# Strided attention feeding two token-mixing layers on one core: the softmax of batches 1 and 2 is transposed two steps behind its scores instead of one

## The chip, the cores and the metric

The kernel runs on one core of a Trainium2 chip. Five engines work side by side, each through its own queue in order: TensorE (PE in the rows; PEld is its weight load), VectorE (DVE), ScalarE (ACT), GpSimd (POOL) and SyncE (SP), which here issues nearly all DMA transfers. The metric is the device time of one execution in microseconds; it is given as the median over several runs, beside the span of one profiled execution.

## The reference

Four batches (B = 4) of 576 tokens and 8 heads of 64 channels go through three layers. All inputs are float32.

```
scores = q k^T / sqrt(64);  heads 0-3 keep 0 <= i-j < 32, heads 4-7 keep j <= i, j = i (mod 32)
attn   = exp(scores - max) / (sum + 1e-9);  x = attn v, heads side by side       (576 x 512)
h = relu(x w_in); u, v = halves of h; v_n = (v - mean) / sqrt(var + 1e-6)
x2 = (u * (w_spatial v_n + b)) w_out                                             (576 x 512)
th = x2 w_theta;  y = w_tok_r (x2 cos th) + w_tok_i (x2 sin th);  s = x2 + y
out = s + relu(s w_ch)
```

The second and third layer are dense; every batch passes through the same weights. The attention is sparse: a local head needs a band of 32 keys per query, and a strided head, after its tokens are permuted, is block diagonal with small triangles.

## The kernel before, in words

**The main work.** Dense products run in float16 in three passes (high x high, low x high, high x low parts), because one float16 pass is not exact enough. For every batch b the generator `main_v(b)` computes v (tiles `v`) and normalizes it into `vn`; `main_mid(b)` computes u (`u`), the spatial product (`sp`), x2 (tiles `x`) and theta (`th`) with sine and cosine (tiles `ta`); `main_end(b)` computes y (`y`) and the last product (`c`). They run in the order v(0), mid(0), v(1), end(0), mid(1), v(2), end(1), and so on, so v of the next batch stands behind th of this one. `main_v(b)` reads the attention's output `xT` of batch b: four chunks of 128 channels (two heads each), each as a high part, written by ScalarE, and a low part, written by VectorE as source minus high part. The weights arrive as raw 64-bit floats; they are turned to float32 and split by ScalarE, VectorE and GpSimd while batch 0 is in `main_mid` (tiles `x2f`, `zf`, `xT_94` as staging, `wx` and `x2h` in between, `wout`, `wth`, `wtok`, `wch` as results).

**The attention of batches 1 and 2** is the generator `attention1(b)` (line 810), in float32. Its blocks of 64 or 54 queries are grouped in eight `quads`: five local (heads 0 to 3), then three strided, of which the middle one mixes two head pairs. A step s does up to four things. `qd_scores` writes the scores and masks of quad s into a PSUM tile `a`, taken from the same three buffers (`pm`) that the tiles u, sp, x, th, v, y and c take. `qd_softmax` (line 745) has VectorE take the maximum (`st`) and subtract it (`sm`), and ScalarE take the exponential in place; `qd_div` divides by the sum on VectorE. `qd_turn` transposes `sm` on TensorE into the one PSUM bank `av`, and ScalarE copies it to `pT`. `qd_px` multiplies `pT` with v into the bank `sc` (strided quads: `sc` and `av`), and `gr_parts` copies the result into `xT`, the high part on ScalarE, then the low part on VectorE. Before, step s held scores(s), turn(s-1) and px(s-2).

**What sets the order.** Python generators are advanced by a clock that counts the columns of the main matmuls: step n of the attention of a batch starts at `ATT_AT[b][0] + n * ATT_AT[b][1]` (line 57: 2.7 + 4.2 n for batch 1, 86.0 + 5.4 n for batch 2). `main_v(b)` is not begun before the attention of b is drained. A list scheduler then orders the instructions of each engine: first come those with the higher priority, and by program order otherwise; calls through `hv`, `ha`, `hg` (line 166) count as 200 instructions earlier (`AHEAD`). Nearly all evacuations of the main work go through these; the maximum and the subtraction of `qd_softmax` did not. DMA transfers wait in one SyncE queue; `load_b(hp)` issues 4 transfers for a local and 13 for a strided pair of v.

All compute is recorded through helper functions, so every row of the profile shows the same line, L107; rows are told apart by their tiles.

Of the kernel before, what the change touches and what calls it, by code (L numbers as in the profile page):

```python
# [14 lines left out]
F32 = mybir.dt.float32  # L15
# [4 lines left out]
ALU = mybir.AluOpType  # L20
# [49 lines left out]
def kernel(  # L70
# [52 lines left out]
    nc = Engines  # L123
# [18 lines left out]
    P = 128  # L142
# [23 lines left out]
    hv, ha, hg = Ahead(nc.vector, AHEAD), Ahead(nc.scalar, AHEAD), Ahead(nc.gpsimd, AHEAD)  # L166
# [12 lines left out]
    att_p = ctx.enter_context(tc.tile_pool(name="att", bufs=1))  # L179
# [43 lines left out]
    def pm(name):  # L223
        return ps_m.tile([P, 2, 512], F32, tag="pm", name=name)

    def pa(tag):
        return ps_a.tile([P, 512], F32, tag=tag, name=tag)

    def pa4(tag):
        return pa(tag).rearrange("p (n k) -> p n k", n=4)  # L230
# [227 lines left out]
    def load_qk(b, hp, q, k, c0, c1, by=None):  # L458
        by = by or nc.sync
        local = hp < 2  # L460
        src = kzl[b, hp] if local else kzs[b, hp - 2]
        k0, k1 = (c0 + STRIDE if c0 else 0, c1 + STRIDE) if local else (c0, c1)
        by.dma_start(q[:, c0:c1], qp[b, hp][:, c0:c1])
        for j in range(2):
            h = slice(64 * j, 64 * j + 64)
            by.dma_start(k[h, k0:k1], src[h, j, k0:k1])
# [155 lines left out]
    def gr_parts(b, local, blocks, xt, by=1):  # L622

        xh = xT[b % 2]
        runs = []
        for i, (hp, blk) in enumerate(blocks):
            if runs and runs[-1][0] == hp and (local or blk < 10):
                runs[-1][3] += 1
            else:
                runs.append([hp, blk, i, 1])  # L630
        for hp, blk, i, n in runs:
            src = xt[:, QB * i:QB * (i + n)]
            if local:
                dst = [xh[:, e, hp, QB * blk:QB * (blk + n)] for e in range(2)]
            else:
                nr = min(3, STRIDE - 3 * blk)
                r0, o = (3 * (blk - blk % by), blk % by) if nr == 3 else (3 * blk, 0)
                dst = [xh[:, e, hp, :].rearrange("p (j r) -> p j r", r=STRIDE)
                       [:, :, r0:r0 + n * nr * (by if nr == 3 else 1)]
                       .rearrange("p j (n t r) -> p j n t r", n=n, r=nr)[:, :, :, o] for e in range(2)]  # L640
                src = src.rearrange("p (n c) -> p n c", c=QB)[:, :, 0:nr * NCLS].rearrange(
                    "p n (r j) -> p j n r", j=NCLS)
            nc.scalar.activation(dst[0], src, AF.Copy)
            nc.vector.tensor_tensor(dst[1], src, dst[0], ALU.subtract)
# [61 lines left out]
    NQ = len(quads)  # L706

    def qd_size(g):
        local, slots = quads[g]
        return local, slots, len(slots), 96 if local else QB  # L710
# [34 lines left out]
    def qd_softmax(g, sc, sm, st):  # L745
        local, slots, ns, w = qd_size(g)
        n = 2 * ns
        sv = sc[:, :, 0:ns * w].rearrange("p j (n c) -> p j n c", c=w)
        mx = st[:, 0, 0:n].rearrange("p (j n) -> p j n", j=2)
        nc.vector.tensor_reduce(out=mx, in_=sv, op=ALU.max, axis=mybir.AxisListType.X)  # L750
        nc.vector.tensor_tensor(sm[:, 0:n * w].rearrange("p (j n c) -> p j n c", j=2, c=w), sv,
                                mx.unsqueeze(3).broadcast_to([P, 2, ns, w]), ALU.subtract)
        nc.scalar.activation(sm[:, 0:n * w], sm[:, 0:n * w], AF.Exp, scale=0.125)

    def qd_div(g, sm, st):

        local, slots, ns, w = qd_size(g)
        n = 2 * ns
        p, sums = sm[:, 0:n * w].rearrange("p (n c) -> p n c", c=w), st[:, 1, 0:n]
        nc.vector.tensor_reduce(out=sums, in_=p, op=ALU.add, axis=mybir.AxisListType.X)  # L760
        nc.vector.tensor_scalar(sums, sums, 1e-9, 1.0 / XS, op0=ALU.add, op1=ALU.mult)
        nc.vector.reciprocal(sums, sums)
        nc.vector.tensor_tensor(p, p, sums.unsqueeze(2).broadcast_to([P, n, w]), ALU.mult)

    def qd_places(g):


        local, slots, ns, w = qd_size(g)
        if local:
            return [f * w for f in range(2 * ns)], lambda j, s: (j * ns + s, 0)  # L770
        odd = ns % 2
        starts = []
        for j in range(2):
            starts += [j * ns * w] * odd + [(j * ns + s) * w for s in range(odd, ns, 2)]
        half = len(starts) // 2
        return starts, lambda j, s: (j * half + (s + odd) // 2, 64 * ((s + odd) % 2) if s or not odd else 0)

    def qd_turn(g, sm, pt, pT):
        local = quads[g][0]
        w, n = (96, P)[not local], len(qd_places(g)[0])  # L780
        for t, c in enumerate(qd_places(g)[0]):
            nc.tensor.transpose(pt[0:w, t, :], sm[:, c:c + w], ident)
        nc.scalar.activation(pT[0:w, 0:n], pt[0:w, 0:n], AF.Copy)

    def qd_px(b, g, v, pT):


        local, slots, ns, w = qd_size(g)
        place = qd_places(g)[1]
        banks = (pa("sc"),) if local else (pa("sc"), pa("av"))  # L790
        held = [[] for _ in banks]
        for s, slot in enumerate(slots):
            for half, (hp, blk) in enumerate(slot):
                e = 0 if local else blk % 2
                m = QB if local else min(CB, S - CB * blk)
                o = QB * len(held[e])
                held[e].append((hp, blk))
                for j in range(2):
                    t, r = place(j, s)
                    q = slice(64 * half, 64 * half + m)  # L800
                    if local:
                        lhs, rhs = v[hp][0:96, blk, 64 * j:64 * j + 64], pT[0:96, t, q]
                    else:
                        assert r == 64 * e
                        lhs, rhs = v[hp][r:r + m, blk // 2, 64 * j:64 * j + 64], pT[r:r + m, t, q]
                    nc.tensor.matmul(banks[e][64 * j:64 * j + 64, o:o + m], lhs, rhs, start=True, stop=True)
        for e in range(len(banks)):
            gr_parts(b, local, held[e], banks[e], len(banks))

    def attention1(b):  # L810
        q, k, v = {}, {}, {}

        def load_a(hp):
            q[hp], k[hp] = kts[hp % 2][:, 0], kts[hp % 2][:, 1]
            load_qk(b, hp, q[hp], k[hp], 0, S)

        def load_b(hp):
            v[hp] = att_p.tile([P, 9, P], F32, tag="vT", name="v32", bufs=2)
            if hp < 2:
                load_vl(b, hp, v[hp])  # L820
            else:
                load_vs(b, v[hp][:, 0:6].unsqueeze(1), (hp,))

        load_a(0)
        load_b(0)
        yield
        load_a(1)
        load_b(1)
        loads = {2: (load_a, 2), 4: (load_a, 3), 5: (load_b, 2), 6: (load_b, 3)}
        un = {}  # L830
        for s in range(NQ + 2):
            def turn():
                sm, pT, st = un[s - 1]
                qd_turn(s - 1, sm, pa4("av"), pT)

            if s == NQ:
                turn()
            if s >= 2:
                sm, pT, st = un.pop(s - 2)
                qd_px(b, s - 2, v, pT)  # L840
            if s < NQ:
                sm = att_p.tile([P, 512], F32, tag="sm", name="sm", bufs=2)
                pT = att_p.tile([P, 4, P], F32, tag="pT", name="pT32", bufs=2)
                st = att_p.tile([P, 2, 8], F32, tag="st", name="st", bufs=4)
                un[s] = (sm, pT, st)
                sc = pm("a1")
                qd_scores(s, q, k, sc)
                qd_softmax(s, sc, sm, st)
            if s in loads:
                f, hp = loads[s]  # L850
                f(hp)
            if 1 <= s < NQ:
                turn()
            if s < NQ:
                qd_div(s, *un[s][::2])
            yield


# [373 lines left out]
    timed([lambda n=n: tok_step(n) for n in range(len(toks))], *CONV_TOK)  # L1232
    timed(sq_parts(wch, w_ch, 2), *CONV_CH)
    atts = [None] + [attention1(b) for b in range(1, N32)] + [attention(b) for b in range(N32, B)]
    for at, f in [(at, lambda n=n: tok_load(*toks[n])) for n, at in enumerate(TOK_AT)] + [
            (at, lambda: next(atts[N32])) for at in PREP_AT]:
# [148 lines left out]
```

## Time and profile before

| | |
|---|---|
| median of 3 runs | 496.44 us (493.58 to 498.56) |
| the profiled execution | 493.71 us, its span 491.9 us |
| TensorE busy | 470.0 us, 96% of the span |
| VectorE, ScalarE, GpSimd busy | 300.8, 268.4, 72.6 us |
| attention of batch 1 in the span | about 36 to 112 us, beside v(0) and mid(0) |
| attention of batch 2 in the span | about 158 to 227 us |

In the profile's page the span is cut in 40 equal slices of 12.3 us. TensorE's share is six to nine tenths in the first eight of them, up to 98 us, and nine tenths or more from there to the last slice. VectorE and ScalarE are mostly five to nine tenths busy up to about 150 us and mostly less than half later, VectorE with exceptions. Where TensorE waits, the trace names the engine and tile whose result came last.

### The profile page before, as it was taken

To read this page: it belongs to the slowest core of one execution; us is meant where nothing else is said; L and a number is where in the kernel's file an instruction comes from. 1 tells how busy PE (TensorE), PEld (TensorE's weight loads), DVE (VectorE), ACT (ScalarE), POOL (GpSimd) and SP (SyncE) were. 2 spreads that over 40 slices of the span, in tenths; PEclk is the share of its full clock that TensorE was granted. 3 is DMA by queue.
4 is the path that set the end of the run, shared out by engine and by line. 5 is a ranking of instruction groups with operands and counts; after the bars stand their busy time and mean duration, and the time that the engine had idled before them with its cause. 6 is when DMAs were issued, how large, how long until landed. Compare 5 with 4: busy or idle time off the path is not lost. (4 is left out here: it accounts for less than half of the span.)

```text
span 491.9 us, 10785 instructions
## 1 busy us (share of the span) xinstructions
PE 470.0 (96%) x4440; PEld 353.6 (72%) x4440; DVE 300.8 (61%) x639; ACT 268.4 (55%) x480; POOL 72.6 (15%) x69
## 2 busy tenths in 40 slices
PE   7889869799999999999999999999999999999996
PEld 5655647567477777777668877777667777777775
DVE  4766987966898655762688778862687121217412
ACT  2657777878974334444955657654952022148202
POOL 2041144120004300111004110021005200210320
PEclk9999979999999999999999999999999999999999
DMA  6887647465890064200282255230360020003502
GB/s 178 284 228 219 206 166 220 161 227 130 220 199 1 0 211 133 59 26 1 49 218 85 57 151 158 45 65 1 47 147 1 2 97 0 1 2 73 121 0 98
DMA packets 71820, 52.72 MB, mean 107 GB/s; under 512 B 50584, under 2 KB 59992, under 8 KB 71770
## 3 DMA queue, kind: packets, MB, share of 16 engines
q1 hardware_dynamic: 71466, 51.42, 38.1%
q8 instruction: 35, 0.57, 0.5%
q10 hardware_dynamic: 304, 0.61, 0.4%
q14 instruction: 15, 0.12, 0.1%
HBM read 35.36 MB, written 4.72 MB: 81 GB/s over the span
## 5 line engine op out<-in xcount | busy, mean ns | idle before, releaser
L107 PE MATMUL y<-wtok,zf 128*128 128x288 f16 x864 | 107.2, 286 | 0.0
L107 PEld LDWEIGHTS <-zf 128*128 128x128 f16 x864 | 84.1, 98 | 22.2 <-issue 1.2
L107 PE MATMUL sp<-wsp,vn 128*128 128x288 f16 x384 | 51.5, 291 | 1.7 <-ACT vn L107 1.7
L107 PE MATMUL u<-xT,win 128*128 128x288 f16 x384 | 50.3, 289 | 2.0 <-DVE sm L107 2.0
L107 PEld LDWEIGHTS <-vn 128*128 128x128 f16 x416 | 41.0, 99 | 12.6 <-ACT vn L107 1.9
L107 PE MATMUL v<-win,xT 128*128 128x512 f16 (+1 forms) x240 | 48.6, 380 | 1.2 <-POOL win L107 0.6
L107 PE MATMUL x<-zf,wout 128*128 128x288 f16 x384 | 49.6, 286 | 0.0
L107 PE MATMUL th<-x2h,wth 128*128 128x288 f16 x384 | 47.8, 286 | 0.0
L107 POOL TENSOR_TENSOR x2h<-x2f,x2h 128x576 f16<-128x576 f32 x19 | 26.2, 1383 | 141.9 <-issue 66.0
L107 PEld LDWEIGHTS <-win 128*128 128x128 f16 x384 | 37.8, 99 | 11.8 <-DVE sm L107 2.3
L107 PE MATMUL c<-x2h,wch 128*128 128x288 f16 x360 | 45.2, 286 | 0.0
L107 PEld LDWEIGHTS <-wth 128*128 128x128 f16 x384 | 37.6, 98 | 9.6 <-issue 0.2
L107 PEld LDWEIGHTS <-wch 128*128 128x128 f16 x384 | 37.5, 98 | 9.2
L107 PEld LDWEIGHTS <-wout 128*128 128x128 f16 x384 | 36.8, 98 | 9.5
L107 PEld LDWEIGHTS <-xT 128*128 128x128 f16 (+1 forms) x240 | 21.0, 100 | 25.7 <-issue 2.8
L107 ACT ACTIVATE x2h<-x2f 128x576 f16<-128x576 f32 (+1 forms) x28 | 20.9, 748 | 24.9 <-DVE x2f L107 23.5
L107 ACT ACTIVATE o<-c 128x576 f32<-128x576 f32 x15 | 9.7, 645 | 34.9 <-PE c L107 34.7
L107 DVE TENSOR_TENSOR ta<-ta,x2f 128x1152 f32<-128x1152 f32 (+1 forms) x17 | 21.7, 1283 | 11.2 <-ACT ta L107 11.2
L107 DVE SCALAR_TENSOR_TENSOR x2f<-y,x2f 128x576 f32<-128x576 f32 x16 | 12.0, 752 | 25.4 <-PE y L107 25.3
L107 POOL TENSOR_TENSOR zf<-u,zf 128x576 f16<-128x576 f32 x8 | 10.2, 1280 | 113.9 <-ACT zf L107 109.4
L107 DVE TENSOR_TENSOR u<-u,sp 128x576 f32<-128x576 f32 x16 | 12.0, 751 | 24.5 <-PE sp L107 24.5
L107 DVE SCALAR_TENSOR_TENSOR o<-x2f,o 128x576 f32<-128x576 f32 (+1 forms) x17 | 12.2, 722 | 23.7 <-ACT o L107 23.7
(146 smaller groups left out, 724.9 us busy)
## 6 DMA issues: line engine op xcount, KB each, us to landing
out_dram<-o SPq DMA_DIRECT2D x15, 288.0 KB
kt<-in_qp_dram SPq DMA_DIRECT2D x8, 288.0 KB
qs<-in_qd_dram SPq DMA_DIRECT2D x8, 288.0 KB
x2f<-in_w_in_dram SPq DMA_DIRECT2D x2, 1024.0 KB
zf<-in_w_in_dram SPq DMA_DIRECT2D x2, 1024.0 KB
xT<-in_w_ch_dram SPq DMA_DIRECT2D x2, 1024.0 KB
kt<-in_kzl_dram SPq DMA_DIRECT2D x8, 152.0 KB
ks<-in_kl_dram SPq DMA_DIRECT2D x4, 304.0 KB
```

The costliest lines, as they stand in the source:

```text
L107: ins = f(*args, **kwargs)
```

## The change

In `attention1` step s now holds px(s-3), scores(s) and turn(s-2), so a batch takes eleven steps instead of ten, on the same clock. For this, `sm` gets four buffers (the tag `ph`, unused at that time, takes every second one), `pT` is taken when it is needed, and the last load of v moves from step 6 to step 7. In `qd_softmax`, the maximum and the subtraction are issued with priority.

```diff
-        nc.vector.tensor_reduce(out=mx, in_=sv, op=ALU.max, axis=mybir.AxisListType.X)
-        nc.vector.tensor_tensor(sm[:, 0:n * w].rearrange("p (j n c) -> p j n c", j=2, c=w), sv,
+        hv.tensor_reduce(out=mx, in_=sv, op=ALU.max, axis=mybir.AxisListType.X)
+        hv.tensor_tensor(sm[:, 0:n * w].rearrange("p (j n c) -> p j n c", j=2, c=w), sv,
                                 mx.unsqueeze(3).broadcast_to([P, 2, ns, w]), ALU.subtract)
...
-        loads = {2: (load_a, 2), 4: (load_a, 3), 5: (load_b, 2), 6: (load_b, 3)}
-        un = {}
-        for s in range(NQ + 2):
-            def turn():
-                sm, pT, st = un[s - 1]
-                qd_turn(s - 1, sm, pa4("av"), pT)
-
-            if s == NQ:
-                turn()
-            if s >= 2:
-                sm, pT, st = un.pop(s - 2)
-                qd_px(b, s - 2, v, pT)
+        loads = {2: (load_a, 2), 4: (load_a, 3), 5: (load_b, 2), 7: (load_b, 3)}
+        un, pTs = {}, {}
+        for s in range(NQ + 3):
+            if s >= 3:
+                qd_px(b, s - 3, v, pTs.pop(s - 3))
             if s < NQ:
-                sm = att_p.tile([P, 512], F32, tag="sm", name="sm", bufs=2)
-                pT = att_p.tile([P, 4, P], F32, tag="pT", name="pT32", bufs=2)
+                sm = att_p.tile([P, 512], F32, tag=("sm", "ph")[s % 2], name="sm", bufs=2)
...
                 qd_scores(s, q, k, sc)
                 qd_softmax(s, sc, sm, st)
...
-            if 1 <= s < NQ:
-                turn()
+            if 2 <= s < NQ + 2:
+                pT = att_p.tile([P, 4, P], F32, tag="pT", name="pT32", bufs=2)
+                pTs[s - 2] = pT
+                qd_turn(s - 2, un[s - 2][0], pa4("av"), pT)
             if s < NQ:
-                qd_div(s, *un[s][::2])
+                qd_div(s, *un[s])
```

VectorE's queue where batch 0's v is normalized, before: `rs` is the chain that ends in 1/sqrt(var), `vr` are the rows of v, `a_797` and `a_868` the scores of steps 2 and 3, `wspt` the last rows of the spatial weights.

```order
L107 SCALAR_TENSOR_TENSOR wspt<-x2f,wspt 1x576
L107 SCALAR_TENSOR_TENSOR rs<-rs 128x5
L107 TENSOR_TENSOR sm<-a_797,st 128x192
L107 TENSOR_SCALAR vr_629<-vr_629,mv,rs 128x512
L107 TENSOR_SCALAR vr_651<-vr_651,mv,rs 128x512
L107 TENSOR_SCALAR vr_698<-vr_698,mv,rs 64x512
```

And with the change (here the scores of step 3 are `a_848`):

```order
L107 TENSOR_SCALAR vr_650<-vr_650,mv,rs 128x512
L107 TENSOR_TENSOR vn<-vr_690,vn 64x512
L107 TENSOR_REDUCE st<-a_848 128x4
L107 TENSOR_TENSOR vn<-vr_628,vn 128x2x512
L107 TENSOR_TENSOR sm<-a_848,st 128x384
L107 SCALAR_TENSOR_TENSOR wspt<-x2f,wspt 1x576
L107 RECIPROCAL st<-st 128x2
L107 TENSOR_TENSOR xT_95<-sc,xT_95 128x256
```

The subtraction of step 3, which frees a `pm` buffer, stands further ahead than its sums; `wspt`, after which SyncE may reuse `x2f`, has gone behind the whole of `vr`.

ScalarE's queue at the end of the attention of batch 1, before: `x_1449` is the last tile of x2, and `xT_95` with 18x4x3 the high part of the last quad, which makes up chunk 3 of `xT`.

```order
L107 ACTIVATE x2h<-x2f 128x576
L107 ACTIVATE xT_95<-sc 128x18x4x3
L107 ACTIVATE xT_95<-av 128x18x4x3
L107 ACTIVATE xT_94<-xT_94 128x1152
L107 ACTIVATE wx<-xT_94 128x1152
L107 ACTIVATE x2f<-x_1449 128x576
```

With the change (`th_1598` is the last of the four theta tiles, `ta_1587` belongs to the third):

```order
L107 ACTIVATE wtok<-wx 128x576
L107 ACTIVATE ta_1587<-ta_1587,halfpi 128x576
L107 ACTIVATE ta_1587<-ta_1587 128x576
L107 ACTIVATE ta_1623<-th_1598 128x576
L107 ACTIVATE xT_95<-sc 128x18x4x3
L107 ACTIVATE xT_95<-av 128x18x4x3
L107 ACTIVATE xT_94<-xT_94 128x1024
```

The two copies have gone from ahead of the theta tiles to behind the evacuation of the last one. On VectorE the two low parts stand likewise right behind the last `ta<-th`.

TensorE's queue in v of batch 1 with the change (`v_1635`, `v_1667`, `v_1707` are its three tiles; before, the 24 matmuls of the first came in one piece, then those of the second):

```order
L107 MATMUL v_1667<-win,xT_95 128x512
L107 LDWEIGHTS xT_95
L107 MATMUL v_1635<-win,xT_95 128x512
L107 LDWEIGHTS xT_95
L107 MATMUL v_1667<-win,xT_95 128x512
L107 LDWEIGHTS xT_95
L107 MATMUL v_1707<-win,xT_95 64x512
```

Ahead of the first row stand 9 matmuls of `v_1635` and 8 of `v_1667`, for the chunks 0 to 2 alone; the next two are the first of each tile on the high part of chunk 3, and behind 5 of `v_1707` the queue needs the low part of chunk 3; 14, 14 and 7 matmuls are left then.

## Rows read from the trace of the kernel before

**Rows 1.** The page: busy us, share of the span and instructions of each engine.
```profile
PE 470.0 (96%) x4440; PEld 353.6 (72%) x4440; DVE 300.8 (61%) x639; ACT 268.4 (55%) x480; POOL 72.6 (15%) x69
```
**Rows 2.** TensorE's waits: tile, releaser: us in total, times, longest us.
```profile
PE av L107 <- ACT zf L107: 2.2, 1, 2.2
PE u L107 <- DVE sm L107: 2.0, 1, 2.0
...
PE av L107 <- DVE rs L107: 1.5, 1, 1.5
PE av L107 <- DVE sm L107: 1.1, 1, 1.1
...
PE av L107 <- ACT pT L107: 0.7, 1, 0.7
```
**Rows 3.** Timeline of TensorE: start, duration, instructions, [idle before, releaser].
```profile
64.37 0.42 PE L107 MATMUL sp<-wsp,vn 128*128 128x288 f16 x2 [1.73 <-ACT vn L107]
...
69.20 4.15 PE L107 MATMUL sp<-wsp,vn 128*128 128x288 f16 x22
...
95.14 0.39 PE L107 MATMUL a<-mask,identb 128*128 128x256 bf16 x2
```
**Rows 4.** Windows: us, busy of PE, PEld, DVE, ACT, POOL, granted clock, DMA.
```profile
65.00:66.00 1.00, 0.00 (x0) 0.00 (x0) 1.00 (x2) 1.00 (x2) 0.67 (x1) 0.50 0.00 0
...
70.00:71.00 1.00, 1.00 (x6) 0.64 (x5) 0.90 (x4) 1.00 (x2) 0.55 (x1) 0.50 0.66 74
...
88.00:90.00 2.00, 0.59 (x5) 0.23 (x3) 2.00 (x3) 1.58 (x2) 0.00 (x0) 1.00 0.16 45
```
**Rows 5.** The chain that ended last: start, us, what.
```profile
317.95 3.43 PE sp L107 x28
...
350.87 11.78 PE v L107 x60
```
**Rows 6.** Timeline of TensorE at th of batch 0, v of batch 1, y of batch 0.
```profile
112.83 12.06 PE L107 MATMUL th<-x2h,wth 128*128 128x288 f16 x96
124.72 11.94 PE L107 MATMUL v<-win,xT 128*128 128x512 f16 x60
136.59 13.65 PE L107 MATMUL y<-wtok,zf 128*128 128x288 f16 x110
```
**Rows 7.** Timeline of ScalarE, from vn of batch 0 to the last theta tile.
```profile
61.79 2.52 ACT L107 ACTIVATE vn<-vr 64x512 f16<-64x512 f32 x3
...
94.84 1.16 ACT L107 ACTIVATE wtok<-wx 128x1152 f16<-128x1152 f32 x1 [1.01 <-DVE wx L107]
...
96.48 0.40 ACT L107 ACTIVATE xT<-sc 128x216 f16<-128x216 f32 x1
...
96.99 1.12 ACT L107 ACTIVATE x2f<-x2f 128x1024 f32<-128x1024 f32 x1
...
100.61 0.63 ACT L107 ACTIVATE sm<-sm 128x512 f32<-128x512 f32 x1 [0.49 <-DVE sm L107]
...
105.58 0.59 ACT L107 ACTIVATE pT<-av 128x512 f32<-128x512 f32 x1
...
120.18 1.17 ACT L107 ACTIVATE ta<-th 128x576 int32<-128x576 f32 x2
...
132.37 0.63 ACT L107 ACTIVATE ta<-th 128x576 int32<-128x576 f32 x1
```
**Rows 8.** Timeline of VectorE: a low part of xT, the last theta tile.
```profile
111.17 0.39 DVE L107 TENSOR_TENSOR xT<-av,xT 128x216 f16<-128x216 f32 x1
...
133.92 0.75 DVE L107 SCALAR_TENSOR_TENSOR ta<-th,ta 128x576 f32<-128x576 f32 x1
```
**Rows 9.** Timeline of SyncE: the second half of w_out is issued.
```profile
59.96 0.39 SPq L107 DMA_DIRECT2D x2f<-in_w_out_dram  x1
```
**Rows 10.** Timeline of TensorE in batch 2, at the transposes of quad 6.
```profile
210.08 0.66 PE L107 MATMUL av<-ident,sm 128*128 128x128 f32 x4 [0.80 <-DVE xT L107]
```
**Rows 11.** Timeline of ScalarE in batch 2, between the parts of quad 6.
```profile
217.94 0.84 ACT L107 ACTIVATE vT<-vs 128x768 f16<-128x768 f32 x1 [0.40 <-PE av L107]
```

More of the change, by code (lines that the diff above doesn't have):

```diff
@@ L828, in attention1 @@
         load_b(1)
-        loads = {2: (load_a, 2), 4: (load_a, 3), 5: (load_b, 2), 6: (load_b, 3)}
-        un = {}
-        for s in range(NQ + 2):
-            def turn():
-                sm, pT, st = un[s - 1]
-                qd_turn(s - 1, sm, pa4("av"), pT)
-            if s == NQ:
-                turn()
-            if s >= 2:
-                sm, pT, st = un.pop(s - 2)
-                qd_px(b, s - 2, v, pT)
+        loads = {2: (load_a, 2), 4: (load_a, 3), 5: (load_b, 2), 7: (load_b, 3)}
[3 more added lines that the diff above has]
+                qd_px(b, s - 3, v, pTs.pop(s - 3))
             if s < NQ:
-                sm = att_p.tile([P, 512], F32, tag="sm", name="sm", bufs=2)
-                pT = att_p.tile([P, 4, P], F32, tag="pT", name="pT32", bufs=2)
+                sm = att_p.tile([P, 512], F32, tag=("sm", "ph")[s % 2], name="sm", bufs=2)
                 st = att_p.tile([P, 2, 8], F32, tag="st", name="st", bufs=4)
-                un[s] = (sm, pT, st)
+                un[s] = (sm, st)
                 sc = pm("a1")
```

## The prediction, made blind

> **What bounds the kernel now.** I read the page first: TensorE is busy for 96% of the span, the others far less [rows 1]. So a gain can only come from TensorE's idle time or from its clock. The list of waits comes next. Six of them lie between 48 and 113 us, where the attention of batch 1 runs beside v(0) and mid(0): three of transposes (`av`: 2.2, 1.5 and 1.1), one of a product (`av` on `pT`, 0.7), one of a u tile for a `pm` buffer that a subtraction frees (2.0) [rows 2], and one of `sp` for the normalized v (1.7) [rows 3]. That is 9.2 us. Third, the windows: from 65 to about 71.2 us the granted clock is 0.50, the 1.2 GHz level, after TensorE had stood still for most of 62.6 to 66.8 us [rows 3, 4]. Its price is in the timeline: 22 matmuls of `sp` took 4.15 us [rows 3], where 28 take 3.43 [rows 5], so 22 should take 2.7; that is 1.45 lost there, and with some u matmuls at the same clock about 2.1. Batch 2 has one such wait of 0.80 [rows 10]. Everything the change can win is thus about 9.2 + 2.1 + 0.8 = 12.1 us, 2.4%.
>
> Then the other engines. Between 48 and 135 us ScalarE and VectorE also convert the weights and are seldom idle; ScalarE evacuates the last theta tile only at 132.37 to 133.0 [rows 7], 8 us after TensorE had finished th and begun v at 124.72 [rows 6]. In this kernel that lateness costs nothing: nothing in v needs it early.
>
> **The change, part by part.** (1) No operation is added or removed: the same transposes, products, exponentials and copies run, at other places. The priority and the fourth `sm` buffer cost nothing by themselves. The 13 transfers of the last v pair move one step later in SyncE's queue, and their product does too, so they keep their lead of two steps.
>
> (2) *Waits that go.* With one more step between division and transposes, the waits of 1.5, 2.2 and 1.1 on `av` go, and the subtraction moved ahead frees the buffer for which u waited 2.0. With the stillness at 64 to 67 us the slow clock should go as well (2.1).
>
> (3) *The wait for v of batch 0 stays.* `sp` still waits for `vn`. In TensorE's new queue from 48.7 us on, 72 matmuls of u at 0.1225 (3.43 / 28 [rows 5]) make 8.8 us, and the scores of steps 2 and 3, two transposes and one product about 2.7, so it is there at 60.2. On VectorE `wspt` and an `xT` have left the chain ahead of `vr`, which brings `vn` forward by about half a microsecond; on ScalarE the wanted one of the three `vn` (2.52 us together [rows 7]) is now the second, another 0.8 or more. So `sp` starts between 62.3 and 64.4; I take 62.6, a wait of 2.4 in place of 1.7. Smaller waits of a few tenths behind it (low parts, `wspt`) make some 0.7.
>
> (4) *Lead at the last scores.* Up to the scores of quad 7, which end at 95.5 [rows 3], the account is: gone 1.5 + 1.7 + 2.0 + 2.2 + 2.1 = 9.5; come 2.4 + 0.7; and one transposition and one product (about 0.9 together) are done later than this point. 9.5 - 3.1 + 0.9 = 7.3; my walk through the queue gives 8.5. I take 8.
>
> (5) *ScalarE's lead at the theta tiles.* Its exponential of quad 7 stood 5 us behind those scores, at 100.61 [rows 7]; the same VectorE work stands between them now. But by the new order it then has more left before the first `ta`: one `wtok`, one conversion of w_th in two parts, and one `pT` more (1.16, 1.12 and another like it, 0.59 [rows 7]), while the `xT` copies of quad 5 come in and those of quad 7 go out (0.40 each, twice). With 0.1 us of overlap each this is 3.6. Of the 19.6 us between 100.61 and 120.18, about 4.5 are ScalarE's waits by the gaps of its timeline; with TensorE further ahead about 0.8 of these go. So the first `ta` comes 8 - 3.6 + 0.8 = 5.2 us earlier than at 120.18, and the last one, behind an unchanged queue, 5.2 earlier than 132.37. Bounds: 3 (the account's 7.3 and no wait less, a further one on GpSimd or a transfer) and 7 (the walk's 8.5 and half of the waits gone).
>
> (6) *What the copies cost where they are now.* TensorE's lead is larger: th would end some 6 us earlier, near 118.7. But v can't use it. Chunk 3 of `xT` is copied behind the last `ta` on ScalarE and behind the last `ta<-th` on VectorE. If that one did not move (133.92 + 0.67), the two low parts (0.39 each, 0.1 overlapped [rows 8]) would be ready at 135.2. Left then are 14 + 14 + 7 matmuls of v. The 60 of v take 11.78 [rows 5]; counting the 12 of the tail as 6, since two run at a time, one is 0.218, and what is left 31.5 x 0.218 = 6.9. v would end at 142.1, where before it ended at 136.6, the start of y [rows 6]: 5.5 lost. With ScalarE 5.2 earlier, it ends at 136.9: **0.3 lost**; with the bounds 7 and 3 of step 5, 1.5 won to 2.5 lost. The new waits are inside v: some 2.7 us before the second tile (its buffer is freed by the third `ta<-th`), and 2 to 2.5 us before chunk 3.
>
> (7) *Batch 2.* The transposes of quad 6 still follow the product of quad 5 after only 8 matmuls and need the same bank `av`, so the 0.80 stays [rows 10]. The transposes of quad 7 now stand behind the product of quad 6, whose copies have a `vT` of 0.84 [rows 11] among them: up to 0.6 more, against 21 matmuls of cover; 0.8 won to 0.6 lost, I take 0.2 lost, since the cover nearly reaches. Its last copies come ahead of the theta tiles, so v of batch 2 has no new wait.
>
> **Sum.** 0.3 + 0.2 = 0.5 us slower: 493.71, the profiled execution, becomes 494.2. The median of the runs, 496.44, stands 2.7 above that execution; by it the forecast is **496.9 us**, no change. About 1% (5 us) is what a measurement of this kernel can tell from no change.
>
> **Weighed against the trace.** The clock was at its lower level from 65 us after two near idle stretches with two matmuls between them [rows 3, 4]; where TensorE was busy for 0.59 of 88 to 90 us it stayed at 1.00 [rows 4]. The new v has two idle stretches, with nine matmuls between them. I count it as staying at 2.4 GHz. The Trainium skill ("TensorE: Matmul & The Clock Gate", Part 1) says that the throttled clock is the default and that only sustained activity releases it; by that rule the second half of v could run at 1.2 GHz, and the sum would be 3.6 instead of 0.5. The trace agrees with the rule as far as its one fall goes; it has no case as busy as this.
>
> **Rivals.** *A, ScalarE keeps up.* If its waits between 92 and 114 us vanish altogether, the last `ta` comes 9 us earlier, v is no longer held, and its end follows th: 118.7 + 11.8 = 130.5, 6 us won, 490.6. For it: ScalarE is busy 55% over all [rows 1]. Against: it shares these microseconds with VectorE, GpSimd and the transfers of the weights, and its queue is in order.
>
> *B, the weights hold ScalarE.* The second half of w_out was issued at 59.96 [rows 9], right behind `wspt`. `wspt` now stands behind `vr` and `vn`, near 65.5, so this transfer starts 5.6 us later, and every raw tile after it uses the same staging and the same SyncE queue. If the delay is handed on to the theta tiles, ScalarE gains nothing, and v ends 5.5 later: 502. It decides if the last `ta` comes at 132 or later. Against: on ScalarE the half tile was taken up only 8 us after its issue, so most of the delay has room.
>
> *C, the slow clock in v.* The mechanism of the paragraph above as this trace shows it: 6.2 us at half speed cost 3.1; 500.0.
>
> **How the numbers follow.** The forecast has 0.62, its own range by the bounds of steps 5 to 7 is 494.1 to 499.5. A has 0.12, B 0.10, C 0.16. The range for 8 in 10 reaches to C on the one side and most of the way to A on the other: 492.0 to 500.5. Faster by over 1% is A where it is full, and a little for the spread of the runs: 0.12. Slower by over 1% is B and a part of C: 0.14. Within 1%: 0.74.
>
> **What would show it.** In the new profile: no wait of `av` on `rs` or `sm` and no u wait for `sm` between 55 and 100 us; the clock at full speed around 65 to 72; `sp` waiting some 2.4 for `vn` near 62.6; th starting 7 us earlier than 112.83; the last `ta<-th` near 127, not 132; waits of v on ScalarE or VectorE of 4 to 6 us together; y starting within 2 us of 136.59. I am wrong if v runs without waits (A), if the last `ta<-th` has not moved (B), or if the clock falls within v (C).

## The result, and the profile after

The changed kernel takes 497.66 us (median of 20 runs, 495.26 to 500.12), the kernel before 494.03 on the same chip: ratio **1.0059**, 95% interval 1.0038 to 1.0080, so 0.6% slower, which is within the 1% that the prediction called no change. The interval does not hold 1, so the loss, though small, is real. The profiled execution took 497.99 us, its span 496.2.

The page's row of busy times, beside [rows 1]:

```profile
PE 473.1 (95%) x4440; PEld 353.8 (71%) x4440; DVE 301.7 (61%) x639; ACT 268.8 (54%) x480; POOL 76.1 (15%) x69
```

TensorE is busy for 3.1 us more (470.0 to 473.1) with the same instructions: that is slower clock, not work. (Experiment 1 below, whose mean granted clock is 0.999, has 467.1.) The list of its waits comes next, beside [rows 2] (tile, releaser: us in total, times, longest):

```profile
PE av L107 <- DVE xT L107: 3.3, 3, 2.6
PE v L107 <- DVE ta L107: 3.1, 2, 2.6
...
PE v L107 <- ACT xT L107: 1.9, 1, 1.9
PE sp L107 <- ACT vn L107: 1.8, 1, 1.8
```

The four kinds of wait at which the change is aimed, `av` on `rs`, `sm` and a late ScalarE, u on `sm`, are gone. In their place stand waits that the kernel before did not have: 5.0 us of v, on theta tiles (`ta`) and on its own input (`xT`), and a longer one of `av`. The timeline of TensorE shows where the time is won and where it is given back; it answers to [rows 3, 6]:

```profile
63.17 0.42 PE L107 MATMUL sp<-wsp,vn 128*128 128x288 f16 x2 [1.82 <-ACT vn L107]
...
65.46 3.73 PE L107 MATMUL sp<-wsp,vn 128*128 128x288 f16 x22
...
89.33 0.39 PE L107 MATMUL a<-mask,identb 128*128 128x256 bf16 x2
...
100.63 0.66 PE L107 MATMUL av<-ident,sm 128*128 128x128 f32 x4 [2.60 <-DVE xT L107]
101.12 4.16 PE L107 MATMUL x<-zf,wout 128*128 128x288 f16 x19
...
121.73 2.11 PE L107 MATMUL v<-win,xT 128*128 128x512 f16 x9
126.39 2.10 PE L107 MATMUL v<-win,xT 128*128 128x512 f16 x9 [2.56 <-DVE ta L107]
130.42 0.60 PE L107 MATMUL v<-win,xT 128*128 128x512 f16 x2 [1.92 <-ACT xT L107]
131.54 9.58 PE L107 MATMUL v<-win,xT 128*64 128x512 f16 x40 [0.51 <-DVE ta L107]
141.04 9.24 PE L107 MATMUL y<-wtok,zf 128*128 128x288 f16 x74
```

TensorE is ahead of the kernel before by 5.8 us at the last scores (95.14 to 89.33) and by 3.0 at the start of v (124.72 to 121.73). At y it is 4.45 behind (136.59 to 141.04): v took 19.3 us instead of 11.9. From y to the end both kernels need the same 355 us. Three queues show why v waits. ScalarE's timeline, beside [rows 7]:

```profile
93.89 0.63 ACT L107 ACTIVATE sm<-sm 128x512 f32<-128x512 f32 x1 [2.01 <-DVE sm L107]
...
116.95 1.21 ACT L107 ACTIVATE ta<-th 128x576 int32<-128x576 f32 x2
...
129.18 0.63 ACT L107 ACTIVATE ta<-th 128x576 int32<-128x576 f32 x1
129.71 0.40 ACT L107 ACTIVATE xT<-sc 128x216 f16<-128x216 f32 x1
129.97 0.39 ACT L107 ACTIVATE xT<-av 128x216 f16<-128x216 f32 x1
```

VectorE's, beside [rows 8]:

```profile
130.73 0.75 DVE L107 SCALAR_TENSOR_TENSOR ta<-th,ta 128x576 f32<-128x576 f32 x1
131.40 0.40 DVE L107 TENSOR_TENSOR xT<-sc,xT 128x216 f16<-128x216 f32 x1
131.69 0.39 DVE L107 TENSOR_TENSOR xT<-av,xT 128x216 f16<-128x216 f32 x1
```

The copies of the last quad stand right behind the last theta tile, and chunk 3 of v can't start before them. And SyncE's [rows 9], on which rival B rested: the second half of w_out went out 7.9 us later than before.

```profile
67.83 0.39 SPq L107 DMA_DIRECT2D x2f<-in_w_out_dram  x1
```

The windows tell the rest of v (us, busy of TensorE with its instructions, granted clock, DMA share, GB/s):

```profile
102.00:104.00 2.00, 2.00 (x10) 0.50 1.02 392
...
132.00:134.00 2.00, 2.00 (x7) 0.52 0.76 187
134.00:136.00 2.00, 2.00 (x7) 0.63 1.00 223
136.00:138.00 2.00, 2.00 (x11) 1.00 0.17 36
```

Behind the waits TensorE ran at the lower level, 1.2 GHz, for most of four microseconds: 7 matmuls of v in two microseconds, where it does 11 at the upper one.

The account of the span, then: between 48 and 141 us the waits were 9.2 us and are 10.5 (0.2 of u, 1.8 of `sp`, 0.9 of products, 2.6 of `av`, 5.0 of v), 1.3 more; the clock takes 3.1 more, with falls near 65, at 102 and in v where there was one. Together that is 4.4, against the 4.3 by which the span is longer.

### The profile page after: what moved, and what is told of

Its sections match the earlier page's. It is cut to its first block, busy times and chain, and to the rows that moved or that the text cites. A ratio compares the mean times of both kernels' runs of the same rounds, so it can differ in the third digit from the quotient of the medians.

```text
span 496.2 us, 10775 instructions
## 1 busy us (share of the span) xinstructions
PE 473.1 (95%) x4440; PEld 353.8 (71%) x4440; DVE 301.7 (61%) x639; ACT 268.8 (54%) x480; POOL 76.1 (15%) x69
## 5 line engine op out<-in xcount | busy, mean ns | idle before, releaser
L107 PE MATMUL v<-win,xT 128*128 128x512 f16 (+1 forms) x240 | 51.0, 388 | 6.1 <-DVE ta L107 3.1
L107 PE MATMUL x<-zf,wout 128*128 128x288 f16 x384 | 50.9, 292 | 0.0
L107 PEld LDWEIGHTS <-wout 128*128 128x128 f16 x384 | 37.8, 100 | 10.3
L107 POOL TENSOR_TENSOR x2h<-x2f,x2h 128x576 f16<-128x576 f32 x19 | 27.3, 1437 | 105.4 <-DVE x2h L107 46.7
L107 DVE TENSOR_TENSOR ta<-ta,x2f 128x1152 f32<-128x1152 f32 (+1 forms) x17 | 21.7, 1283 | 11.8 <-ACT ta L107 11.8
L107 POOL TENSOR_TENSOR zf<-u,zf 128x576 f16<-128x576 f32 x8 | 11.3, 1417 | 109.2 <-ACT zf L107 109.2
L107 DVE TENSOR_TENSOR x2h<-x2f,x2h 128x576 f16<-128x576 f32 x13 | 10.1, 775 | 26.7 <-ACT x2h L107 26.6
```

What stands on the lines that cost most here:

```text
L107: ins = f(*args, **kwargs)
```

## The experiments

All ratios are to the kernel before, run on the same chip beside each kernel (494.31 us for experiments 1, 3, 4 and 5, 494.74 for the others). The experiments ran on two chips, so kernels of different experiments are compared by their ratios.

**1. The copies of the last quad ahead of the theta tiles.** The one thing that the theory blames is taken away, in the changed kernel:

```
-            nc.scalar.activation(dst[0], src, AF.Copy)
-            nc.vector.tensor_tensor(dst[1], src, dst[0], ALU.subtract)
+            (ha if ahead else nc.scalar).activation(dst[0], src, AF.Copy)
+            (hv if ahead else nc.vector).tensor_tensor(dst[1], src, dst[0], ALU.subtract)
 ...   with ahead = (b == 1 and g == NQ - 1), given by qd_px
```

> The changed kernel, but the xT copies of the last quad of batch 1 (ScalarE) and their low parts (VectorE) are given out with priority, so that they stand ahead of the theta tiles instead of behind the last one. If v is held by these copies (the theory: they cost the waits of 1.9 and 0.5, and the slow clock in the 40 matmuls behind them another 2.4), v has no wait before chunk 3, those 40 matmuls take 7.2 instead of 9.58, y starts near 136, and the time is 492.5 to 494 against 497.7. If the clock falls because of the wait of 2.6 before the second tile alone, only the two waits go: 495.3. If ScalarE's queue is what counts, whatever stands in it, the copies push the theta tiles back by as much and the time stays within 0.7 of the changed kernel's.

Measured: 491.41 us (490.59 to 493.13), ratio 0.9942 (0.9922 to 0.9961). That is below every figure expected, by the ratios 5.8 us faster than the changed kernel, and 2.9 faster than the kernel before. ScalarE's timeline in this kernel:

```profile
114.75 0.43 ACT L107 ACTIVATE xT<-sc 128x216 f16<-128x216 f32 x1
115.00 0.43 ACT L107 ACTIVATE xT<-av 128x216 f16<-128x216 f32 x1
...
116.50 1.22 ACT L107 ACTIVATE ta<-th 128x576 int32<-128x576 f32 x2
...
128.75 0.64 ACT L107 ACTIVATE ta<-th 128x576 int32<-128x576 f32 x1
```

and TensorE's:

```profile
121.19 11.94 PE L107 MATMUL v<-win,xT 128*128 128x512 f16 x60
133.06 17.20 PE L107 MATMUL y<-wtok,zf 128*128 128x288 f16 x139
```

The last theta tile is no earlier than in the changed kernel, once the 0.9 us by which this execution is ahead from the scores of step 1 on (47.63 against 48.55) are taken off: 128.75 + 0.9 against 129.18, and yet v runs through: 60 matmuls in one row, no wait, 11.9 us instead of 19.3. All three waits of v went, not only the two that I had named. The one for `ta` was a consequence too: with chunk 3 late, the scheduler had put nine matmuls of the second tile ahead of it, and these needed a buffer that a theta tile still held. With chunk 3 at hand the first tile's 24 matmuls stand first in the queue again, as in the kernel before, and no wait is left, so the buffer is free by then.

What won the 2.9 us against the kernel before is less clear. In this profiled execution TensorE stands idle for 21.7 us of the span, nearly as long as before (21.9), and is busy for 2.9 less (467.1 to 470.0), with no fall of the clock between 58 and 146 us. In the other five executions, with a mean granted clock of 0.989 to 0.993, it is still 490.9 to 493.1 us. How the gain divides between waits and clock is not shown.

**2. The same place of the copies, in the kernel before.** The mirror of it: nothing is turned later, nothing has priority, only these copies are tied to the place behind the last theta tile.

```
+            while m == 3 and last:      # in z_chunk, behind ta<-th of the last tile
+                gr_parts(*last.pop(0), (ta1.ins.name, ta2.ins.name))
 ...   gr_parts ties its two instructions behind the two named
```

> The kernel before, with one thing done to it: the xT copies of the last quad of batch 1 and their low parts are put behind the last theta tile's evacuation (ta on ScalarE, ta<-th on VectorE), as the changed kernel has them; the scheduler then gives v the changed kernel's order too. Nothing is turned later and nothing has priority. The theory, by the prediction's own step 6 (ScalarE's lead 0): v has waits for ta and xT, y starts at 142.1 instead of 136.6, and the time is 5.5 above the kernel before, 499.8; with the slow clock in v as in the changed kernel, 502. If the place of the copies is not the cause, but the later turning, the time stays within 1 of 494.3.

Measured: 500.62 us (499.73 to 503.60), ratio 1.0136 (1.0105 to 1.0166): by the medians 5.9 us slower than the kernel before. TensorE's timeline:

```profile
125.62 2.11 PE L107 MATMUL v<-win,xT 128*128 128x512 f16 x9
129.76 3.51 PE L107 MATMUL v<-win,xT 128*128 128x512 f16 x9 [2.03 <-DVE ta L107]
133.79 0.60 PE L107 MATMUL v<-win,xT 128*128 128x512 f16 x2 [0.51 <-ACT xT L107]
134.90 7.94 PE L107 MATMUL v<-win,xT 128*64 128x512 f16 x40 [0.51 <-DVE ta L107]
142.77 7.40 PE L107 MATMUL y<-wtok,zf 128*128 128x288 f16 x59
```

TensorE's queue in v has the changed kernel's order (9, 9, 1, 1, 5, 14, 14 and 7 matmuls). Step 6 had put the end of v at 142.1 for just this case; y starts at 142.77. The place of the two copies and their low parts alone costs more than the whole change.

**3. Turning later, without the priority.**

```
-        hv.tensor_reduce(out=mx, ...
-        hv.tensor_tensor(sm[...
+        nc.vector.tensor_reduce(out=mx, ...
+        nc.vector.tensor_tensor(sm[...
```

> The changed kernel without the priority: maximum and subtraction are given out in their turn, the exponentials are turned two steps behind. If the delay in turning is what moves the waits into v, y starts as late as in the changed kernel and the time is 496.5 to 498.5, with the u wait of 2.0 for the scores' buffer back near 64 us. If the priority is what costs (it puts four operations ahead of those that make vn, and wspt late, and with it the second half of w_out), sp starts a microsecond earlier, w_out is asked for near 61 and the time is 493 to 495.

Measured: 495.18 us (493.56 to 499.44), ratio 1.0012 (0.9984 to 1.0040): no difference from the kernel before, between the two expectations and decided by something else than either. Here the scheduler gives the copies out ahead of the theta tiles (ScalarE 118.65, the first `ta` 120.19), and v has no wait (125.80, 60 matmuls in a row). What the later turning wins is lost earlier:

```profile
63.48 0.42 PE L107 MATMUL sp<-wsp,vn 128*128 128x288 f16 x2 [2.78 <-ACT vn L107]
...
67.71 4.37 PE L107 MATMUL sp<-wsp,vn 128*128 128x288 f16 x22 [1.63 <-DVE vn L107]
...
102.33 1.11 PE L107 MATMUL av<-ident,sm 128*128 128x128 f32 x4 [3.21 <-DVE xT L107]
```

The u wait that I expected is not there; waits for `vn` are, 4.4 us together. Over the whole span TensorE is idle for 1.4 us less than in the kernel before (20.5 against 21.9), but busy for 2.6 more (472.6 against 470.0): the granted clock is 0.50 for most of 64 to 71 us and from 102 to 108.

**4. The priority, without turning later**, in the kernel before:

```
-        nc.vector.tensor_reduce(out=mx, ...
-        nc.vector.tensor_tensor(sm[...
+        hv.tensor_reduce(out=mx, ...
+        hv.tensor_tensor(sm[...
```

> The kernel before with the priority alone: exponentials are turned one step behind, as before. If the queue theory holds, v has its chunk 3 in time, since the last copies stand ahead of the theta tiles as before, so what TensorE wins by the freed buffer (the u wait of 2.0, perhaps the slow clock of 2.1) is kept: 490.5 to 493 against 494.0. If the priority costs by the later wspt and w_out, the time is 495 to 497.

Measured: 495.18 us (493.39 to 498.67), ratio 1.0023 (1.0002 to 1.0044). No gain. The theory had asked for 490.5 to 493; the time lies in the second range, that of a priority that costs. v has its chunk 3 in time, as the theory says (60 matmuls in a row at 126.15). But the u wait of 2.0 is gone only for waits of `sp` for `vn` and of u to take its place:

```profile
63.33 0.42 PE L107 MATMUL sp<-wsp,vn 128*128 128x288 f16 x2 [0.76 <-ACT vn L107]
...
64.81 0.52 PE L107 MATMUL u<-xT,win 128*128 128x288 f16 x2 [1.06 <-ACT u L107]
...
67.58 3.78 PE L107 MATMUL sp<-wsp,vn 128*128 128x288 f16 x15 [2.25 <-DVE vn L107]
```

The longest is for VectorE's low part of `vn`, which takes 3.11 us there (64.41 to 67.52) instead of 1.22 in the kernel before; the last section comes back to it. `wspt` and the second half of w_out are late too (issued at 64.45, before 59.96); no wait shown here is put down to them.

So neither half wins by itself, and neither moves the copies behind the theta tiles; only the two together do. Together, and with the copies in time (experiment 1), they win 2.9 us.

**5. Batch 1 alone.** The changed kernel, with a choice by batch:

```
+        if b == 1:
             (the changed loop over s)
+        else:
+            (the loop of the kernel before)
```

> The changed kernel with the new order in batch 1 alone; batch 2 turns its exponentials one step behind, as before, with the priority in both. If the loss lies in batch 1 (from the start of y in batch 1 to the end both kernels take 355.2 to 355.3), this is as slow as the changed kernel, 497.7 within 0.7. If batch 2 lost what I took at 0.2 or more, it is 1 to 3 faster.

Measured: 497.10 us (496.05 to 498.26), ratio 1.0051 (1.0031 to 1.0072), beside 1.0059 for the whole change. The priority stays in both batches here. The loss is batch 1's; the later turning in batch 2 is neutral within what these intervals can tell, about 1 us. In the changed kernel its one wait of 0.80 [rows 10] has become two small ones:

```profile
220.75 0.66 PE L107 MATMUL av<-ident,sm 128*128 128x128 f32 x4 [0.29 <-DVE xT L107]
...
230.73 0.63 PE L107 MATMUL av<-ident,sm 128*128 128x128 f32 x4 [0.36 <-DVE xT L107]
```

**6. TensorE kept at work in the waits of v.** In the changed kernel, the nine matmuls ahead of each wait are done twice, and the second time starts the sums afresh.

```
+                    for c in range(3 if b == 1 and t == 0 else 0):
+                        for n, (xe, we) in enumerate(PASS):
+                            nc.tensor.matmul(ps[:, t, :], xh[:, xe, c, ...], win[:, we, c, DM:2 * DM], ...)
```

> The changed kernel, with TensorE kept at work in the two waits of v of batch 1: the nine matmuls ahead of each wait (chunks 0 to 2 of the first and of the second tile) are done twice, the first time for nothing. 18 matmuls more, some 4.0 us of work in waits of 2.6 and 1.9 + 0.5. If the 40 matmuls behind the waits are slow (9.6 instead of some 7.4) because TensorE stood still before them, the granted clock stays at 1.00 through v, they take 7.4, and the time is 1.5 to 2.2 below the changed kernel, 495.5 to 496.2. If the clock has another cause, or if the slowness is not the clock, the time is that of the changed kernel, 497.7, or up to 1 more.

Measured: 497.87 us (495.82 to 499.20), ratio 1.0048 (1.0025 to 1.0071). By the times this can't be told from the changed kernel (1.0059); the gain expected, 1.5 to 2.2 us off that, would be 1.0014 to 1.0029, at the lower end of the interval. The profiled execution of it, 495.82 us, does what the theory says:

```profile
121.05 4.05 PE L107 MATMUL v<-win,xT 128*128 128x512 f16 x18
125.70 3.61 PE L107 MATMUL v<-win,xT 128*128 128x512 f16 x16 [0.60 <-DVE ta L107]
129.72 9.04 PE L107 MATMUL v<-win,xT 128*128 128x512 f16 x44 [0.41 <-ACT xT L107]
138.70 11.57 PE L107 MATMUL y<-wtok,zf 128*128 128x288 f16 x93
```

The granted clock is 1.00 in every window from 120 to 142 us, and v takes 17.65 us instead of 19.31, with 18 matmuls more. One execution is not a proof, and this one is the fastest of nine; the median does not follow it. Two others, with a mean granted clock of 0.998 and 0.999, took 497.36 and 498.01 us, so a clock that hardly fell is not enough for the gain: what the clock costs in v is left open.

**7 and 8. Two tries for more**, both from the kernel of experiment 1: the priority for the `xT` copies of all quads of batch 1, and for the two VectorE rows of `wspt`.

```
 7:  ahead = (b == 1), in place of (b == 1 and g == NQ - 1)

 8:
-        nc.vector.scalar_tensor_tensor(wspt[0:TL, 1, :], ...
-        nc.vector.scalar_tensor_tensor(wspt[96:97, 1, :], ...
+        hv.scalar_tensor_tensor(wspt[0:TL, 1, :], ...
+        hv.scalar_tensor_tensor(wspt[96:97, 1, :], ...
```

> The kernel of the first experiment (491.4), with the priority on the xT copies of every quad of batch 1, not of the last alone. The largest wait left there is that of the transposes for low parts of xT, 2.6 us near 100. If they are late because conversions stand ahead of them on VectorE, that wait shrinks and the time is 489 to 490.5. If ScalarE's and VectorE's queues are full there, the copies push the exponentials back and it is 491 to 493.

> The kernel of the first experiment (491.4), with wspt's two rows on VectorE given out with priority too, so that the second half of w_out, whose staging they free, is asked for some 5 us earlier again. If the late w_out (rival B) holds ScalarE by a part of the delay, the first ta comes 1 to 2 us earlier; v is no longer held by it, so the time gains little, 490.5 to 491.4. If wspt ahead of vn costs, sp starts up to 1 later: 491.4 to 492.4.

Measured: 491.54 us (490.75 to 493.26), ratio 0.9938 (0.9915 to 0.9960), and 491.95 us (490.89 to 493.91), ratio 0.9943 (0.9922 to 0.9964). Neither moves anything against 0.9942. In the first the wait of `av` near 100 is no shorter (2.98 against 2.61). In the second w_out goes out at 63.19 instead of 66.92, though that execution is 2.7 us behind at the first half (59.42, not 56.73), and nothing is faster for it; `sp` now waits 3.67 us instead of 1.83. In this kernel v does not wait for ScalarE, so it can't show whether the late w_out, rival B, adds to ScalarE's lateness in the changed one: that stays open.

## Why the prediction was right, and where not

The sign, the size class and the mechanism held: what TensorE won in the attention was given back in v, behind two copies that now stand after the last theta tile. Experiments 1 and 2 show it from both sides. The forecast was 0.5 us slower; it is 3.6 slower by the medians, so the sum was too small by 3.1. By the prediction's own signs, y should have started within 2 us of 136.59 and did so 4.45 later, and the clock fell within v, which it had named as showing it wrong.

Two agreements are luck. The 496.9 us stands near the measured 497.66 because 0.5 was added to a median of three runs, 496.44, where twenty give 494.03. And the 3.6 that the prediction gives for a slow clock in v was 3.1 for the clock and 0.5 for the rest; in the profile the clock's part in v is 1.6, and the 2.0 by which ScalarE's lead is smaller is the larger one.

- **Steps 1 to 3: right in the main, the clock of step 2 not.** The waits named are gone. `sp` was forecast at 62.6 behind a wait of 2.4; it starts at 63.17 behind one of 1.82, in an execution that is 0.62 behind at the scores of step 1 already. The lower clock at 65 us did not go altogether: 22 matmuls of `sp` take 3.73, against 4.15 before and the 2.7 I counted. That the priority costs nothing by itself, in step 1, is not borne out: alone it brings the waits for `vn` of experiment 4.
- **Step 4, lead of 8 us at the last scores: too large.** It is 5.8, or 6.4 with the 0.62. In this execution the slow clock near 65 us is a part of what is missing: ten u matmuls take 2.23 us there, 1.39 in experiment 1. In that one, with no slow clock, the lead is the same, since `sp` then meets waits of 0.40 and 0.34, and products waits of 0.70, 0.54 and 0.34: 2.3 us of small waits, where I had put 0.7.
- **Step 5, ScalarE's lead of 5.2 at the theta tiles: mis-sized, and the term that failed most.** It is 3.2. The first `ta` comes 3.2 earlier (120.18 to 116.95), the last one too (132.37 to 129.18), at the lower bound of 3. The exponential of quad 7 was 6.7 earlier (100.61 to 93.89); from there to the first `ta` ScalarE took 23.1 us instead of 19.6, 3.5 more, where I had 2.8. So of the 2.0 that are missing, 1.3 come from step 4's lead of 8 and 0.7 from step 5's own count.
- **Step 6: the formula was right, its input not.** It says 5.5 lost less ScalarE's lead: 5.5 - 3.2 = 2.3, and experiment 2 puts the 5.5 itself at 5.9 by the medians. The waits, 2.6 before the second tile and 1.9 + 0.5 before chunk 3, are those forecast at 2.7 and 2 to 2.5.
- **Step 7: not contradicted.** 0.2 forecast; experiment 5 can't tell so little from nothing, and from y to the end both profiles take the same 355 us.
- **Rival C happened, beside the forecast.** The clock did fall in v. The 40 matmuls took 9.58 us, in experiment 2 the same 40 in the same order 7.94: 1.6 lost, about half of the 3.1 that I had for it. 2.3 + 1.6 makes 3.9 of the 4.45 by which y is late. (The clock's falls at 65 and 102 us are in the account of the span, but not in this sum: by step 6 v's end is set by ScalarE's queue, and a TensorE that came earlier would have waited longer in v.) With v busy for 1.60 of 126 to 128 us, 0.50 of 128 to 130 and 1.07 of 130 to 132, the granted clock was 0.52 from 132 to 134 and 1.00 again from 136. The Trainium skill ("TensorE: Matmul & The Clock Gate", Part 1) has it that the slow clock is the default and activity releases it; this fall and rise agree.
- **Rival A** failed as stated, ScalarE did not keep up. Its time, 490.6, is near that of experiment 1, but it stood for 6 us won against 496.44, and experiment 1 wins 2.9: moving two copies frees v from ScalarE's queue without making ScalarE earlier, and brings half of what A promised. **Rival B** failed: w_out was issued 7.9 us late, and the last `ta` came at 129.2, not after 132; whether the delay took a part of ScalarE's lead is open.

## What to carry to other kernels

When TensorE is brought forward, look up what the other in-order queues hold between its new place and its next input: an operation that had been early by luck can fall behind a long block that it used to precede, and a list scheduler makes that choice without a warning. The place of two copies of 0.4 us each, with their low parts on VectorE, was worth 6 us, and giving them priority turned a change that lost 0.6% into one that wins 0.6%. Two edits that each win nothing may still win together, so a test of each alone does not settle the pair.

## What the runs showed of the hardware

**The same program piece meets either clock.** In the kernel of experiment 1 the transposes near 100 us wait as long as in the changed kernel, behind the same instructions, and the 19 matmuls behind them run at full speed:

```profile
99.73 0.66 PE L107 MATMUL av<-ident,sm 128*128 128x128 f32 x4 [2.61 <-DVE xT L107]
100.23 2.49 PE L107 MATMUL x<-zf,wout 128*128 128x288 f16 x19
```

In the changed kernel it is 4.16 us for the 19, at a granted clock of 0.50, behind a wait of 2.60. So the length of a wait does not by itself tell whether the clock falls. It also differs from run to run of one program: of the 20 runs of the changed kernel, the four with a mean granted clock of 0.997 took 495.3 to 496.3 us, the eight with 0.986 or less 496.8 to 500.1.

**VectorE and GpSimd slow each other.** In the changed kernel two operations of VectorE meet GpSimd's low part of `vn` (the timelines of VectorE and of GpSimd):

```profile
63.94 1.22 DVE L107 TENSOR_TENSOR vn<-vr,vn 128x1024 f16<-128x1024 f32 x1
...
65.66 2.11 DVE L107 SCALAR_TENSOR_TENSOR wspt<-x2f,wspt 1x576 f16<-1x576 f32 x1
```

```profile
64.15 3.00 POOL L107 TENSOR_TENSOR vn<-vr,vn 128x1024 f16<-128x1024 f32 x1 [1.25 <-ACT vn L107]
```

In the kernel before, where these two run clear of GpSimd's `vn`, the three took 1.22, 0.76 and 2.23 us. So VectorE's `vn`, which started first, lost nothing; GpSimd's, which started behind it, took 0.77 more; and the one-row `wspt`, which started while GpSimd still ran, took 1.35 more. In experiment 3 GpSimd starts first, and VectorE's `vn` pays:

```profile
64.83 2.82 DVE L107 TENSOR_TENSOR vn<-vr,vn 128x1024 f16<-128x1024 f32 x1
```

```profile
64.45 2.12 POOL L107 TENSOR_TENSOR vn<-vr,vn 128x1024 f16<-128x1024 f32 x1 [1.25 <-ACT vn L107]
```

It is the same in experiment 4 (3.11 us), and in both it is what `sp` waits for. The Trainium skill ("SBUF — State Buffer", Who interferes with whom) has it that a VectorE operation with two inputs in SBUF contends with a GpSimd operation that reads SBUF; these rows agree, with 1.60 and 1.89 us more for VectorE's `vn`.
